# Second tokens' casts ahead of the first superblock's evictions, and two convolution parts in every step of the third superblock

## The chip, the cores and the metric

The kernel runs on one core of one Trainium2 chip. The metric is the device time of one execution in microseconds; the time before is the median of three runs. The profile is of one further execution.

## The reference

Eight sequences of 4096 tokens with 192 channels each go through a causal convolution of seven taps (a softmax of a learned weight per head, so one set of taps per channel), and the result goes through a two-layer network of 2048 hidden units with a squared ReLU between the layers:

```
w   = softmax(weight)                       # 8 heads x 7 taps, repeated over 24 channels each
x'  = sum over k of w[k] * x[t - 6 + k]     # zeros ahead of each sequence
h   = x' @ w_in                             # 32768 x 192 @ 192 x 2048
g   = s * relu(h)**2 + b
out = g @ w_out                             # 32768 x 2048 @ 2048 x 192, float32
```

## The kernel before

**Tiles.** The 32768 tokens are cut into 32 superblocks `n` of 1024 tokens, each of two blocks `j` of 512. The 2048 hidden units are cut into eight pairs `p` of 2 x 128. One step `(n, j, p)` computes the hidden units of pair `p` for one block. Channels lie on the partitions: 128 of them in an A tile, the other 64 in a B tile that holds both blocks' halves. Every float32 operand of a matmul is split into a high part and a low part, and three products (high x low, high x high, low x high) are accumulated.

**Work of a step.** `first(n, j, p)` issues 18 matmuls into `h` (line 547), in three groups of six: those on `sA`, then those on `tB` and `wB`, then those on `wA`. Here `sA` is the split A convolution, `wA` the same with its two partition halves exchanged, `tB` and `wB` the B convolution and its exchange. `relu` (L570) and `square` (L578) run on ScalarE; a cast to the high part (L580) on VectorE or ScalarE; the low part `ql` (L584) on VectorE. The results are put in a queue, and `second(...)` multiplies them by `w_out` two steps later (`LAG` is 2). For superblock 0 this is `second_whole` (L628 to L637), for superblock 1 `second_split` (L659), from superblock 2 on the loop of L714, with the last 64 output channels done for a whole superblock at once in `second_B` (L733), called by `batch(n - 1)` in step `(n, 0, 1)`.

**Evictions.** At `p` = 7 the accumulators leave PSUM: in superblock 0 by two ScalarE instructions and one VectorE instruction for each block (L641, L643, L645), in superblock 1 by four ScalarE instructions (L680, L683), later by L721 and L722. The output of superblock 0 and of block `(1, 0)` waits in SBUF for a bias that is known only in step `(2, 0, 0)`: `biases()` sums it with matmuls (L528) and VectorE (L530), GpSimd adds it to six tiles (L534), and these are written out (L535). The evictions of `(1, 1)` reuse the SBUF tiles of these outputs.

**The convolution ahead of time.** `Tokens(n).steps()` is a generator that issues the convolution and the casts of superblock `n` in small parts: for block 0 seven parts of the A convolution on VectorE (L174, L176) and two parts of its split (L191 on ScalarE; L193 on VectorE, with the exchange by DMA); then seven parts of the B convolution for both blocks and two or three parts of its split; then nine parts of the A tile of block 1. That is 27 parts for superblock 1, 28 for each other one, of which the first 19 are all that block 0 needs (the last of them exchanges `wB` by DMA, L184 and L185). For superblock 1 the B split is `split_B_at_once`: its first part casts the high part on ScalarE (L222), copies it into `tB` and `wB` (L227, twice) and subtracts on VectorE (L229, twice), and sets `begun`. `convolve(k)` issues the next `k` parts of the coming superblock; it stops early where a convolution ends, and the parts it still owes are added to the next call. `finish(block)` issues whatever parts are still missing for that block; every superblock calls it at the head of step `(n, j, 0)`.

**Order.** VectorE, ScalarE and TensorE run in the order in which the program names the instructions; a context called `in_order` fixes this. The loads of `x` are put as early in the SyncE queue as their buffers allow (`headed`), about two superblocks ahead. Superblock 0 is written out in `head()` and `pair(p)`; after `pair(7)` a loop issues the six outstanding `second_whole` groups, of which the last two carry the evictions of superblock 0. Then the steps of superblock 1 begin.

**What the counts give before.** When step `(2, 0, 0)` begins, 23 of the 28 parts of superblock 2 are issued. Its 16 steps call `convolve` with 1, 2, 1, 2 and so on, 24 parts in all: 5 for the rest of superblock 2, 19 for superblock 3. The 19th is issued in step `(2, 1, 7)`. From superblock 3 on, each superblock calls for 30 parts (`FIRST`), two more than the 28 needed.

Of the kernel before, what the change touches and what calls it, by code (L numbers as in the profile page):

```python
# [45 lines left out]
def conv_attention_then_squared_relu_mlp(  # L46
# [25 lines left out]
    NPAIR = weights64.shape[0]  # L72
# [308 lines left out]
    tok = {0: Tokens(0)}  # L381
# [117 lines left out]
    def column_sums(k):  # L499

        if k == 1:
            nc.gpsimd.memset(sumB[:, 0:DB], 0.0)
            for h in range(2):
                hi, lo = (splitB[h][:, :, k, :].bitcast(F32) for k in range(2))
                half = WB[:, h * NPAIR // 2 : (h + 1) * NPAIR // 2]
                nc.vector.tensor_tensor(half.rearrange("p a b d -> p (a b) d"), hi, lo, op=ALU.add)
        for o, w, w0 in (
            (sumA, W[:, k, :, CI:CB].bitcast(F32), W[:, 0, :, CI:CB].bitcast(F32)),
            (sumB[:, DB:].rearrange("p (j d) -> p j d", j=2), WB[:, k], WB[:, 0]),
        ):  # L510
            nc.vector.tensor_tensor(o, w0 if k == 1 else o, w, op=ALU.add)
        if k == NPAIR - 1:
            a, b = sumA, sumB
            nc.vector.tensor_tensor(a[:, 0, :], a[:, 0, :], a[:, 1, :], op=ALU.add)
            nc.vector.tensor_tensor(a[:, 0, 0:P], a[:, 0, 0:P], a[:, 0, P:], op=ALU.add)
            nc.vector.tensor_tensor(b[:, DB:P], b[:, DB:P], b[:, P:], op=ALU.add)
# [5 lines left out]
    def biases():  # L522

        pb = ps_h.tile([P, 2, BLK], F32, name="h")
        for k, cols in enumerate((sumA[:, 0, 0:P], sumB[:, 0:P])):
            for i in range(2):
                r = slice(i * HB, (i + 1) * HB)
                nc.tensor.matmul(pb[:, i, k : k + 1], cols[r], bb[r], start=True, stop=True)  # L528
        nc.scalar.copy(bias[:, 0:2], pb[:, 0, 0:2])
        nc.vector.tensor_tensor(bias[:, 0:2], bias[:, 0:2], pb[:, 1, 0:2], op=ALU.add)  # L530
        nc.vector.tensor_copy(bias[0:DB, 2:3], bias[DB:P, 1:2])
        for o, to, k in unbiased:
            rows = slice(0, o.shape[0])
            nc.gpsimd.tensor_scalar(o, o, bias[rows, k : k + 1], None, op0=ALU.add)  # L534
            nc.sync.dma_start(to, o)  # L535


    def first(n, j, p, meanwhile=None):
        h = ps_h.tile([P, 2, BLK], F32, name="h")
        halves = [tok[n].half(j, i) for i in range(2)]  # L540

        def both(w, part, at, start, stop):

            for i in range(2):
                chunk = halves[i][at]
                rows = slice(i * HB, (i + 1) * HB)
                nc.tensor.matmul(  # L547
                    h[:, i, :], w_in(w, p, chunk[0], rows), chunk[part], start=start, stop=stop
                )

        for at in (0, 2, 1):
            both(0, 1, at, at == 0, False)
            both(0, 2, at, False, False)
            both(1, 1, at, False, at == 1)
            if meanwhile and at == 0:
                meanwhile()
        return h
# [8 lines left out]
    def relu(h):  # L566
        g = count[0]
        count[0] += 1
        q = room_for(F32)
        nc.scalar.activation(q, h, AF.Relu)  # L570
        return q, g

    def squares(h, cast):
        return square(relu(h), cast)

    def square(at, cast):
        q, g = at
        nc.scalar.activation(q, q, AF.Square)  # L578
        qh, ql = split_place(g)
        cast(qh, q)  # L580
        return q, qh, ql
# [7 lines left out]
    def put(n, j, p, pair):  # L589
        if n >= OLD:  # L590
            kept[n, j, p] = pair[0]
        queue.append((n, j, p, *lows(*pair)))
# [3 lines left out]
    def banks():  # L596
        return [ps_o.tile([P, BLK], F32, name=f"acc{k}") for k in (1, 2)]
# [129 lines left out]
    def second_B(n, j, accs):  # L727

        for p in range(NPAIR):
            q = kept.pop((n, j, p))  # L730
            for r in (slice(0, HB), slice(HB, P)):
                for i in range(2):
                    nc.tensor.matmul(  # L733
                        accs[r.start // HB][i * DB : (i + 1) * DB], WB[r, p, i, :], q[r, i, :],
                        start=p == 0, stop=p == NPAIR - 1, skip_group_check=True,
                    )
        return accs
# [42 lines left out]
    def start_tokens(n):  # L780
        if n < NSUP:
            tok[n] = Tokens(n)
            tok[n].load()
# [7 lines left out]
    def convolve(k):  # L791


        k += owed[0]
        while k and coming[0] in tok:
            try:
                stop = next(tok[coming[0]].todo)
            except StopIteration:
                coming[0] += 1
                continue  # L800
            k -= 1
            if stop:
                break
        owed[0] = k if coming[0] in tok else 0

    def pair(p):

        ha, hb = first(0, 0, p), first(0, 1, p)
        if p + 1 < NPAIR:
            if p not in TWICE:  # L810
                wide[p + 1].rest()
            ahead, between = 0, CONV[p] // 4
        else:
            ahead, between = CONV[p] // 2, CONV[p] // 4
        convolve(ahead)
        def magnitudes():
            if p + 2 < NPAIR:
                wide[p + 2].magnitudes()

        qa = relu(ha)  # L820
        if p in TWICE:

            magnitudes()
            qb = relu(hb)
        qa = square(qa, nc.scalar.copy)
        if p not in TWICE:
            magnitudes()
        put(0, 0, p, qa)
        if p + 2 < NPAIR:
            wide[p + 2].top()  # L830
        convolve(between)
        if p not in TWICE:
            qb = relu(hb)
        qb = square(qb, nc.scalar.copy)
        if p + 2 < NPAIR:
            wide[p + 2].his()
        if p + 1 in TWICE:
            wide[p + 2].rest()
        put(0, 1, p, qb)
        convolve(CONV[p] - ahead - between)  # L840


    def batch(n):

        a = second_B(n, 0, banks())
        convolve(FIRST[2])
        evict_B(n, 0, a)
        a = second_B(n, 1, banks())
        convolve(FIRST[3])
        evict_B(n, 1, a)  # L850
# [3 lines left out]
    def step(n, j, p):  # L854
        if p == 0:
            tok[n].finish(j)
            if j == 0:
                with headed():
                    start_tokens(n + 1)
            else:  # L860
                tok.pop(n - 1)
        h = first(n, j, p)
        put(n, j, p, squares(h, nc.scalar.copy if n == OLD and p % 2 else nc.vector.tensor_copy))
        if (n, j) == (1, 1):
            if p < NPAIR - 1:
                column_sums(p + 1)
            convolve(1)
        elif n <= OLD:
            convolve(3 if n == 1 else 1 + p % 2)
        else:  # L870
            convolve(FIRST[p] if j == 0 and p < 2 else 1)
        if (n, j, p) == (2, 0, 0):
            biases()
        if (n, j, p) == steps[-1]:
            a = second_B(n, 0, banks())
            h = ps_h.tile([P, 2, BLK], F32, name="h")
            b = second_B(n, 1, [h[:, i, :] for i in range(2)])
            evict_B(n, 0, a)
            last_B(n, 1, b)
            for item in queue:  # L880
                second(*item)
        while queue and len(queue) > LAG + (
            queue[0][2] == 0 and queue[0][0] <= OLD and queue[0][:2] not in ((1, 0), (OLD, 1))
        ):
            if (n, j, p) == steps[-1]:
                break
            second(*queue.pop(0))
        if n > OLD and (j, p) == (0, 1):
            batch(n - 1)

    with in_order(nc.vector, nc.scalar, nc.tensor):
        with in_order(nc.sync):
            head()
        headed = last_of(nc.sync)
        for p in range(NPAIR):
            if p > 1:
                if p + 3 < NPAIR:
                    with headed():
                        fetch(p + 3)
                pair(p)  # L900
            if p > 0 and p not in TWICE:
                while len(queue) > (LAG if p < NPAIR - 1 else 0):
                    second(*queue.pop(0))
        for s_ in steps:
            if s_[0]:
                step(*s_)
# [43 lines left out]
```

## Time and profile before

| | |
|---|---|
| median of 3 runs | 2240.92 us (2239.67 to 2241.11) |
| the profiled execution's own time | 2240.58 us |
| span from its first to its last instruction | 2238.8 us |
| mean granted TensorE clock | 0.998 |
| TensorE matmuls busy | 2222.3 us (99%) |
| VectorE busy | 1734.5 us (77%) |
| ScalarE busy | 1315.0 us (59%) |
| GpSimd busy | 310.9 us (14%) |

In the profile PE is TensorE's matmuls and PEld its weight loads, DVE is VectorE, ACT is ScalarE, POOL is GpSimd, SP is SyncE, which issues the DMAs. A row of the timeline gives the start in us from the first instruction, the duration in us, engine, line, operation, what is written and read, the count of merged instructions, and in brackets the idle time of the engine just before with what ended it. A row of the chain of work that ended last gives start, duration, engine (or DMA), tile, line and count. A row of a stretch (from:to) gives its length, then the busy time and instruction count of PE, PEld, DVE, ACT and POOL, then the granted clock as a share of full speed, and the DMA share and rate.

### The profile page before, as it was taken

To read this page: it belongs to the slowest core of one execution; us is meant where nothing else is said; L and a number is where in the kernel's file an instruction comes from. 1 tells how busy PE (TensorE), PEld (TensorE's weight loads), DVE (VectorE), ACT (ScalarE), POOL (GpSimd) and SP (SyncE) were. 2 spreads that over 40 slices of the span, in tenths; PEclk is the share of its full clock that TensorE was granted. 3 is DMA by queue.
4 is the path that set the end of the run, shared out by engine and by line. 5 is a ranking of instruction groups with operands and counts; after the bars stand their busy time and mean duration, and the time that the engine had idled before them with its cause. 6 is when DMAs were issued, how large, how long until landed. Compare 5 with 4: busy or idle time off the path is not lost.

```text
span 2238.8 us, 44630 instructions
## 1 busy us (share of the span) xinstructions
PE 2222.3 (99%) x19334; PEld 1611.6 (72%) x19334; DVE 1734.5 (77%) x1988; ACT 1315.0 (59%) x1418; POOL 310.9 (14%) x205
## 2 busy tenths in 40 slices
PE   9998999999999999999999999999999999999999
PEld 6787667777777877777777777777777777777776
DVE  8797677877778787777887787877778877878754
ACT  8757555655555655556555566555565555665554
POOL 0013111011111111101111101111011111111110
PEclk9999999999999999999999999999999999999999
DMA  5012121112211111111112112121111121121110
GB/s 179 21 45 69 53 62 50 49 45 62 58 48 48 53 52 49 53 51 45 55 51 57 48 44 57 45 57 51 51 48 53 48 62 46 46 58 39 43 30 17
DMA packets 46165, 117.49 MB, mean 52 GB/s; under 512 B 7760, under 2 KB 8016, under 8 KB 45968
## 3 DMA queue, kind: packets, MB, share of 16 engines
q1 hardware_dynamic: 45824, 114.50, 18.4%
q8 instruction: 151, 2.47, 0.5%
q14 instruction: 46, 0.38, 0.1%
q10 hardware_dynamic: 144, 0.13, 0.0%
HBM read 31.64 MB, written 25.17 MB: 25 GB/s over the span
## 4 chain that ended last, share of the span: by engine, by line
PE 97%; DVE 2%; ACT 1%; DMA 0%; issue 0%; POOL 0%; SPq 0%; DVEq 0%; ACTq 0%
PE h L547 46%; PE acc L714 29%; PE acc L733 18%; PE acc L659 1%; PE acc L629 0%; PE acc L635 0%; PE acc L637 0%; PE h L733 0%; PE acc L636 0%; DVE accA L176 0%; DVE ql L584 0%; ACT q L570 0%; PE acc L628 0%; DMA wB<-tB 0%; PE acc L631 0%
## 5 line engine op out<-in xcount | busy, mean ns | idle before, releaser
L570 ACT ACTIVATE q<-h 128x1024 f32<-128x1024 f32 x512 | 526.4, 1028 | 580.1 <-PE h L547 579.0
L584 DVE TENSOR_TENSOR ql<-q,qh 128x1024 fp32r<-128x1024 f32 x498 | 663.9, 1333 | 60.2 <-ACT qh L580 9.1
L580 DVE CAST qh<-q 128x1024 fp32r<-128x1024 f32 x482 | 337.6, 700 | 379.3 <-ACT q L578 375.9
L714 PE MATMUL acc<-qh,W 64*128 64x512 f32 x3816 | 588.7, 387 | 1.5 <-ACT outs L680 1.5
L578 ACT ACTIVATE q<-q 128x1024 f32<-128x1024 f32 x512 | 543.6, 1062 | 16.0
L547 PE MATMUL h<-sA,W 64*128 64x512 f32 x3072 | 436.9, 389 | 0.0
L547 PE MATMUL h<-tB,W 64*128 64x512 f32 x1536 | 432.0, 387 | 4.7 <-DVE tB L208 2.8
L547 PE MATMUL h<-wB,W 64*128 64x512 f32 x1536 | 432.3, 388 | 4.2 <-DMA wB<-tB 4.1
L547 PE MATMUL h<-wA,W 64*128 64x512 f32 x3072 | 433.4, 387 | 0.0
L714 PEld LDWEIGHTS acc<-qh,W 64*128 64x128 f32 x3816 | 357.7, 184 | 78.2 <-ACT outs L680 1.9
L733 PE MATMUL acc<-q,WB 64*64 64x512 f32 x3776 | 412.1, 591 | 0.0
L714 PE MATMUL acc<-ql,W 64*128 64x512 f32 x1908 | 371.7, 386 | 0.6 <-DVE ql L584 0.6
L547 PEld LDWEIGHTS h<-sA,W 64*128 64x128 f32 x3072 | 285.8, 184 | 84.3 <-issue 24.7
L547 PEld LDWEIGHTS h<-wA,W 64*128 64x128 f32 x3072 | 289.1, 185 | 60.7
L733 PEld LDWEIGHTS acc<-q,WB 64*64 64x64 f32 x3776 | 141.5, 133 | 254.7 <-issue 254.7
L176 DVE SCALAR_TENSOR_TENSOR accA<-xA,tap,accA 128x512 f32<-128x512 f32 x378 | 315.8, 835 | 6.1
L547 PEld LDWEIGHTS h<-tB,W 64*128 64x128 f32 x1536 | 282.9, 184 | 46.3 <-DVE tB L208 3.3
L547 PEld LDWEIGHTS h<-wB,W 64*128 64x128 f32 x1536 | 283.0, 184 | 25.9 <-DMA wB<-tB 5.1
L723 POOL TENSOR_TENSOR outs<-outs 128x512 f32<-128x512 f32 x59 | 96.6, 1638 | 1242.0 <-ACT outs L722 1242.0
L714 PEld LDWEIGHTS acc<-ql,W 64*128 64x128 f32 x1908 | 179.0, 184 | 38.7 <-DVE ql L584 1.0
L176 DVE SCALAR_TENSOR_TENSOR accB<-xB,tap,accB 128x512 f32<-128x512 f32 x186 | 163.9, 881 | 5.6
L743 ACT ACTIVATE outs<-acc,bias,sb 128x512 f32<-128x512 f32 x59 | 45.9, 778 | 159.3 <-PE acc L733 159.3
(144 smaller groups left out, 959.1 us busy)
## 6 DMA issues: line engine op xcount, KB each, us to landing
wA<-sA SPq DMA_DIRECT2D x126, 256.0 KB, 3.7
outT<-outs SPq DMA_DIRECT2D x63, 256.0 KB, 2.0
wB<-tB SPq DMA_DIRECT2D x60, 256.0 KB, 3.4
xA<-in_xA SPq DMA_DIRECT2D x24, 515.0 KB, 3.6
outT<-outs SPq DMA_DIRECT2D x65, 128.0 KB, 2.3
xB<-in_xB SPq DMA_DIRECT2D x32, 259.0 KB, 3.0
outs<-outs SPq DMA_DIRECT2D x61, 128.0 KB, 2.4
outs<-in_w SPq DMA_DIRECT2D x7, 768.0 KB, 6.5
```

The source lines that it names most:

```text
L176: nc.vector.scalar_tensor_tensor(acc, src, w[:, k : k + 1], acc, op0=ALU.mult, op1=ALU.add)
L547: nc.tensor.matmul(h[:, i, :], w_in(w, p, chunk[0], rows), chunk[part], start=start, stop=stop)
L570: nc.scalar.activation(q, h, AF.Relu)
L578: nc.scalar.activation(q, q, AF.Square)
L580: cast(qh, q)
L584: nc.vector.tensor_tensor(ql, q, qh.bitcast(F32), op=ALU.subtract)
L659: nc.tensor.matmul(accs[to + 2 * i][0:cols], w(f, r), q[r, f % 2, :], start=start and f == 0, stop=stop and f == NF - 1,)
L714: nc.tensor.matmul(accs[i], w(f, r), q[r, f % 2, :], start=f == 0 and lo == 0, stop=f == ends[i] and lo == 2,)
L723: nc.gpsimd.tensor_tensor(o, o, o2, op=ALU.add)
L733: nc.tensor.matmul(accs[r.start // HB][i * DB : (i + 1) * DB], WB[r, p, i, :], q[r, i, :], start=p == 0, stop=p == NPAIR - 1, skip_group_c ...
L743: nc.scalar.activation(o, accs[0], AF.Identity, scale=sb, bias=bias[:, 1:2])
```

## The change

Two edits. In the loop over superblock 0's pairs, `tok[1].finish(0)` is called right after `pair(7)`, ahead of the loop that issues the last six `second_whole` groups; when step `(1, 0, 0)` calls it again, there is nothing left to do. The one part that it issues there is the first one of `split_B_at_once` (L222, L227 twice, L229 twice), since `pair(7)` has issued the whole B convolution already. And `convolve` in the steps of superblock 2 is called with 2 each time, 32 in all, instead of 1 and 2 in turn.

```
@@ step(n, j, p)
         elif n <= OLD:
-            convolve(3 if n == 1 else 1 + p % 2)
+            convolve(3 if n == 1 else 2)
@@ loop over the pairs of superblock 0
                 pair(p)
+            if p == NPAIR - 1:
+                tok[1].finish(0)
             if p > 0 and p not in TWICE:
                 while len(queue) > (LAG if p < NPAIR - 1 else 0):
                     second(*queue.pop(0))
```

By the counts, superblock 3 has 11 parts when block `(2, 1)` begins, its 19th is issued in step `(2, 1, 3)`, and 26 are issued when step `(3, 0, 0)` begins, with one owed.

More of the change, by code (lines that the diff above doesn't have):

```diff
@@ L868, in step @@
         elif n <= OLD:
-            convolve(3 if n == 1 else 1 + p % 2)
+            convolve(3 if n == 1 else 2)
         else:
@@ L900, in conv_attention_then_squared_relu_mlp @@
                 pair(p)
+            if p == NPAIR - 1:
+                tok[1].finish(0)
             if p > 0 and p not in TWICE:
```

## The prediction

> **What bounds the kernel.** I read the page first: busy times, then the chain of work that ended last. Then the stretches, to find where TensorE is not full.
>
> ```profile
> PE 2222.3 (99%) x19334; PEld 1611.6 (72%) x19334; DVE 1734.5 (77%) x1988; ACT 1315.0 (59%) x1418; POOL 310.9 (14%) x205
> PE 97%; DVE 2%; ACT 1%; DMA 0%; issue 0%; POOL 0%; SPq 0%; DVEq 0%; ACTq 0%
> 101.00:165.00 64.00, 64.00 (x570) 51.31 (x570) 60.43 (x85) 35.23 (x38) 5.10 (x3) 1.00 0.17 44
> 182.00:200.00 18.00, 18.00 (x162) 14.84 (x160) 14.56 (x17) 14.38 (x15) 1.61 (x1) 1.00 0.25 76
> ```
>
> TensorE is the bound, and the matmuls are not touched. So the change can win only in holes of PE: 2238.8 - 2222.3 = 16.5 us, and besides them the time that a lowered clock adds to busy matmuls. Three holes lie where the edits work, at 91, 173 and 219 us, and a small one at 468 us.
>
> **First edit, the casts at 88 to 94 us.**
>
> ```profile
> 68.18 0.97 PE L547 MATMUL h<-sA,W 64*128 64x512 f32 x6
> ...
> 69.67 0.86 PE L547 MATMUL h<-wA,W 64*128 64x512 f32 x6
> ...
> 87.68 0.74 DVE L176 SCALAR_TENSOR_TENSOR accB<-xB,tap,accB 128x512 f32<-128x512 f32 x1
> 88.46 0.69 ACT L641 ACTIVATE outs<-acc,sb 128x512 f32<-128x512 f32 x1 [1.96 <-PE acc L637]
> 90.62 0.97 PE L547 MATMUL h<-sA,W 64*128 64x512 f32 x6
> 92.15 0.62 ACT L222 CAST hiB<-accB 128x512 fp32r<-128x512 f32 x1
> 93.44 0.62 ACT L227 CAST wB<-hiB 64x512 fp32r<-64x512 f32 x1
> 93.47 0.50 PE L547 MATMUL h<-tB,W 64*128 64x512 f32 x1 [1.88 <-ACT tB L227]
> 96.91 1.02 ACT L570 ACTIVATE q<-h 128x1024 f32<-128x1024 f32 x1 [2.85 <-PE h L547]
> 101.28 0.39 PE L659 MATMUL acc<-qh,q 64*128 64x512 f32 x2
> 95.00:96.00 1.00, 1.00 (x8) 0.84 (x6) 0.00 (x0) 0.00 (x0) 0.00 (x0) 0.50 0.00 0
> ```
>
> The B convolution ends at 87.68 + 0.74 = 88.42, but ScalarE does four evictions from 88.46 on, and the casts start only at 92.15. TensorE has its six `sA` matmuls from 90.62, then stands 1.88 us, and afterwards runs at clock 0.50. With the edit L222 starts at 88.46. The three casts take 92.15 to 94.06, 1.9 us; so `tB` and `wB` are cast by 90.4, and the two subtractions on VectorE, which start when L222 ends, are done by then too. TensorE asks for them at 91.4 (0.8 us after 90.62): no wait, and no clock loss. Undisturbed, a `first` takes 69.67 + 0.86 - 68.18 = 2.35 us to its last result, so `h` is complete at 92.97. Late next are the evictions: the four take 92.15 - 88.46 less the idle 0.88 between them, 2.8 us, and now end at 90.4 + 2.8 = 93.2. The ReLU queued behind them starts at 93.2 and not at 96.91: 3.7 us earlier. VectorE's two L645 end by 94; what follows on VectorE waits for the square at 95.3. The accumulators that the evictions free are wanted at 96.8 (90.62 + three `first` of 2.04). No DMA moves: the first part of this split exchanges nothing.
>
> The bounds: all that is lost here is 101.28 - 96.8 = 4.5 us; nothing, if VectorE (60.43 of 64.00 us busy behind it) is already the pace. I take 3.7, since the ReLU releases ScalarE, VectorE and so TensorE alike, and all three move by it.
>
> **Second edit, the hole at 219 to 232 us.** In the chain:
>
> ```profile
> 212.14 2.04 PE h L547 x18
> ...
> 215.54 2.06 PE h L547 x18
> ...
> 224.32 3.46 DMA wB<-tB
> ...
> 232.01 2.07 PE h L547 x18
> ```
>
> A step takes 215.54 - 212.14 = 3.40 us. Two steps after 215.54 would be 222.34; the trace has 232.01: 9.7 us are lost, to the last B parts (issued in step (2,1,7)), their exchange by DMA and the clock after it. With two parts in each step the 19th part falls into (2,1,3), four steps or 13.6 us earlier, against a lateness of 9.7. All 9.7 go. The exchanges move in SyncE's queue by as much; they are 3.46 us each and have 10 us to spare, even behind an output that waits. The `x` loads only come earlier, as their buffers come free.
>
> Eight parts more run in this superblock, and eight fewer later. Behind 182 us VectorE works 14.56 of 18.00 us, 2.75 us in a step of 3.40. One more part in every second step adds half of 0.75, giving 3.1: it fits. What if not, see below.
>
> **The hole at 468 us.** The `second_B` batches mark the superblocks in the chain; the last row is from the view of who waited for whom, PE alone, 235 to 2200 us:
>
> ```profile
> 372.66 13.89 PE acc L733 x128
> ...
> 441.22 13.89 PE acc L733 x128
> ...
> 510.78 13.89 PE acc L733 x128
> PE acc L714 <- DVE ql L584: 0.6, 1, 0.6
> ```
>
> 68.56 us is the rule, but 69.56 the one from 441.22. There, in step (6,0,2), seven parts come at once, two of a split and five of a convolution, because `convolve` stopped at a convolution's end before and owed the rest. The wait for `ql` is the only one of L714 behind 235 us. By the count, the lead of two parts per superblock makes this pattern in superblock 6 alone; with eight parts more, superblock 3 enters as superblock 7 does now, all but one part, and superblocks 4 on are as 8 on are now, which take 68.56. Gain 1.0 (bounds 0 and 1.0).
>
> **What the second edit costs at 166 to 186 us.**
>
> ```profile
> 165.91 0.74 DVE L176 SCALAR_TENSOR_TENSOR accA<-xA,tap,accA 128x512 f32<-128x512 f32 x1
> 166.57 0.15 DVE L530 TENSOR_TENSOR bias<-bias,h 128x2 f32<-128x2 f32 x1
> 166.82 10.64 POOL L534 TENSOR_SCALAR outs<-outs,bias 128x512 f32<-128x512 f32 x6 [26.13 <-DVE bias L530]
> 172.34 0.78 ACT L680 ACTIVATE outs<-acc,bias,sb 128x512 f32<-128x512 f32 x1 [2.53 <-DMA outT<-outs]
> 174.41 0.73 PE L714 MATMUL acc<-qh,W 64*128 64x512 f32 x4 [1.50 <-ACT outs L680]
> 177.44 1.72 POOL L684 TENSOR_TENSOR outs<-outs 128x512 f32<-128x512 f32 x1
> 178.04 2.19 DVE L584 TENSOR_TENSOR q<-q 128x1024 fp32r<-128x1024 f32 x1
> 179.12 2.27 POOL L688 TENSOR_TENSOR outs<-outs 128x512 f32<-128x512 f32 x1
> 180.59 1.88 DVE L584 TENSOR_TENSOR ql<-q,qh 128x1024 fp32r<-128x1024 f32 x1 [0.35 <-ACT qh L580]
> 181.72 1.90 POOL L693 TENSOR_TENSOR outs<-outs 64x512 f32<-64x512 f32 x1 [0.29 <-DMA outs<-outs]
> 182.40 1.77 DVE L193 TENSOR_TENSOR sA<-accA,sA 128x512 fp32r<-128x512 f32 x1
> 183.87 0.39 PE L714 MATMUL acc<-ql,W 64*128 64x512 f32 x2
> 193.66 1.23 DVE L584 TENSOR_TENSOR ql<-q,qh 128x1024 fp32r<-128x1024 f32 x1 [1.33 <-ACT qh L580]
> 201.60 0.68 DVE L193 TENSOR_TENSOR sA<-accA,sA 128x512 fp32r<-128x512 f32 x1
> 173.00:174.00 1.00, 0.00 (x0) 0.00 (x0) 0.00 (x0) 1.00 (x3) 1.00 (x1) 1.00 0.63 248
> 279.57 1.79 DVE L176 SCALAR_TENSOR_TENSOR accB<-xB,tap,accB 128x512 f32<-128x512 f32 x1
> ```
>
> Times here are those of the trace before, the 3.7 left out. First, in step (2,0,0) a second L176 stands ahead of the bias addition L530. It delays L530, and with it POOL's additions, the output's DMA, the evictions L680 and the matmuls at 174.41, by 0.75 us: the hole becomes 2.3 us.
>
> Second, the split L193 and the first part of the next A convolution (L174) move from behind the L584 at 180.59 to ahead of it. POOL works there. L193 took 1.77 beside POOL, 0.68 alone. After its predecessor ends at 178.04 + 2.19 + 0.75 = 181.0, I let L193 wait for L688 (181.39 + 0.75) and end at 182.8, L174 wait for L693 and end at 184.3, and L584 end at 185.5. TensorE wants this `ql` at 183.87 + 0.75 = 184.6: 0.9 us lost. Uncontended L584 would end at 181.0 + 0.7 + 0.5 + 1.2 = 183.4 and nothing would be lost. The Trainium skill, "SBUF — State Buffer", section "Who interferes with whom", says that a VectorE instruction with two SBUF inputs and a GpSimd instruction that reads SBUF exclude each other for the whole instruction; by it the loss is the 0.9, without it 0, and the 1.77 against 0.68 agrees with it. Later steps absorb the rest: the added part sits where VectorE stands idle 1.33 us.
>
> Cost 0.75 + 0.9 = 1.7 (bounds: 0.7 and 4.1, the latter with the clock of the third rival).
>
> **The sum.** -3.7 - 9.7 - 1.0 + 1.7 = -12.7 us. The profiled execution took 2240.58, 0.3 below the median and 1.8 above its span; so 2227.9 against it, and 2228.2 against the median of 2240.92. I forecast 2228.
>
> **Rivals.** 0.2% of this time, 4.5 us, is about what a measurement can tell from no change: the line is 2236.4.
> 1. VectorE is the pace of superblock 1, and the first edit gives nothing: 60.43 of 64 us speaks for it; against it, TensorE is full throughout. 2228 + 3.7 = 2232.
> 2. VectorE falls behind in parts of superblock 2 (each added part unabsorbed, 8 x 0.75 = 6): 2234. The idle 1.33 speaks against it.
> 3. The longer hole at 173 lowers the clock. After 1.50 us of idleness it stayed 1.00, after 1.88 us at 91 it fell to 0.50, so 2.3 us may trip it. The price by the rows of 91 us is what that hole lost beyond the wait: 4.5 - (93.47 - 91.4) = 2.4, giving 2230.6; most of it runs beside the `ql` waits above, so nearer to 2229. The Trainium skill, "TensorE: Matmul & The Clock Gate", section "What's actually happening", lets the clock fall only after an idle window of about 3.4 us. By that rule 2.3 us trips nothing and the sum stays; the fall after 1.88 us disagrees with so long a window.
> 4. Slower: VectorE saturates over the whole of superblock 2 through contention with POOL. The tipping point is 6.8 us of VectorE work in two steps; it is 5.5 now and 6.25 with the change, so four parts would have to cost 0.14 us more each. At the 1.79 of the row at 279.57 each costs 1.04 more: 6.25 + 4.2 - 6.8 = 3.6 us for each of 8 pairs of steps, 29 us lost; 2240.6 + 29 - 3.7 - 9.7 - 1.0 = 2255. Against it: POOL is busy 1.61 of 18.00 us behind 182.
> 5. The edit does nothing at 88 us because the casts are not what TensorE waits for: the row at 93.47 names L227, so this is the first rival's time again.
>
> **Chances.** The forecast with or without the third rival, 2226 to 2230.6: 0.72. First (and fifth): 0.11. Second: 0.08. Some of these together, up to 2237: 0.06. Fourth: 0.03. The range from 2225.5 to 2234 leaves out less than 2 in 10. Faster by over 0.2%: 0.92; within: 0.05; slower: 0.03.
>
> **What would show it.** L222 ahead of L641 and no wait of PE at `tB` near 91, the clock at 1.00 from 94 to 98; near 217 us (219 less 3.7, plus 1.7) no wait for `tB` or `wB` and steps of 3.40 through into superblock 3; the PE wait behind L680 longer than 1.50 and a new wait for `ql` some 10 us later; all batches 68.56 apart. A VectorE wait of PE in every step from 180 to 215, or in superblock 1, would make the prediction wrong.

## The result, and the profile after

The changed kernel takes 2227.94 us (median of 6 runs, 2226.98 to 2228.08) against 2240.84 us (median of 6, 2239.67 to 2241.11): ratio 0.9942, 95% interval 0.9929 to 0.9955. It is 12.9 us faster, and 2228 was forecast. Its profiled execution took 2227.96 us, span 2226.2 us, mean clock 0.999.

The page, first the busy times:

```profile
PE 2218.1 (100%) x19334; PEld 1610.4 (72%) x19334; DVE 1744.4 (78%) x1988; ACT 1314.9 (59%) x1418; POOL 309.6 (14%) x205
```

TensorE now leaves 2226.2 - 2218.1 = 8.1 us idle, where it left 16.5. The rest of the gain is in the busy time, 2218.1 us where it was 2222.3 for the same 19334 matmuls: a matmul at the lowered clock counts as busy, and for longer (the four of L714 behind the hole at 172 us take 1.22 us at the low clock here, 0.73 at the full one in e4 below).

The casts at 88 us, in the timeline of ScalarE and TensorE (start, duration, engine, line, what, count, idle time before), with the clock at 95 us from the stretches and the start of superblock 2 from the chain of work that ended last:

```profile
88.61 0.62 ACT L222 CAST hiB<-accB 128x512 fp32r<-128x512 f32 x1 [1.96 <-DVE accB L176]
89.91 0.62 ACT L227 CAST wB<-hiB 64x512 fp32r<-64x512 f32 x1
90.55 0.69 ACT L641 ACTIVATE outs<-acc,sb 128x512 f32<-128x512 f32 x1
90.79 0.97 PE L547 MATMUL h<-sA,W 64*128 64x512 f32 x6
91.60 0.39 PE L547 MATMUL h<-tB,W 64*128 64x512 f32 x1
93.46 1.03 ACT L570 ACTIVATE q<-h 128x1024 f32<-128x1024 f32 x1
95.00:96.00 1.00, 1.00 (x12) 0.81 (x10) 0.39 (x1) 0.97 (x2) 0.00 (x0) 1.00 0.00 0
156.26 2.06 PE h L547 x18
```

The casts stand ahead of the evictions L641, the matmul on `tB` has no idle time in brackets, the clock stays at 1.00, and the ReLU starts at 93.46 instead of 96.91. The first step of superblock 2, which began at 159.74 before, begins at 156.26; this execution was 0.17 late already at the `sA` matmuls (90.79 against 90.62), so the edit brings 3.48 + 0.17 = 3.65 us.

The hole where superblock 2 begins, in the timeline and the stretches (from:to, length, busy time and count of PE, PEld, DVE, ACT, POOL, then the granted clock):

```profile
163.88 0.15 DVE L530 TENSOR_TENSOR bias<-bias,h 128x2 f32<-128x2 f32 x1
169.67 0.78 ACT L680 ACTIVATE outs<-acc,bias,sb 128x512 f32<-128x512 f32 x1 [3.33 <-DMA outT<-outs]
171.75 1.22 PE L714 MATMUL acc<-qh,W 64*128 64x512 f32 x4 [2.30 <-ACT outs L680]
172.00:173.00 1.00, 1.00 (x6) 0.81 (x8) 0.00 (x0) 1.00 (x2) 1.00 (x2) 0.50 0.35 84
175.00:176.00 1.00, 1.00 (x12) 0.84 (x10) 0.97 (x2) 0.97 (x2) 1.00 (x2) 0.91 0.37 86
177.34 1.51 POOL L693 TENSOR_TENSOR outs<-outs 64x512 f32<-64x512 f32 x1 [0.72 <-DMA outs<-outs]
177.62 1.77 DVE L193 TENSOR_TENSOR sA<-accA,sA 128x512 fp32r<-128x512 f32 x1
178.21 1.53 PE L714 MATMUL acc<-q,W 64*128 64x512 f32 x12
179.71 1.21 DVE L584 TENSOR_TENSOR ql<-q,qh 128x1024 fp32r<-128x1024 f32 x1
182.06 0.40 PE L714 MATMUL acc<-ql,W 64*128 64x512 f32 x2
178.00:196.00 18.00, 18.00 (x162) 15.42 (x160) 16.30 (x20) 13.59 (x14) 0.84 (x1) 1.00 0.38 104
```

The idle time behind L680 is 2.30 us (1.50 before), and now the clock falls to 0.50 for a good 3 us behind it. The wait for `ql` that the prediction placed here is not there: L584 ends at 179.71 + 1.21 = 180.92, and TensorE takes its result at 182.06. Behind that, VectorE works 16.30 of 18.00 us, 3.08 us in a step of 3.40, without holding up TensorE.

Step (2,0,5), the start of superblock 3, and the batches that mark the superblocks, in the chain:

```profile
179.74 2.04 PE h L547 x18
...
213.74 2.04 PE h L547 x18
220.54 2.04 PE h L547 x18
223.94 13.89 PE acc L733 x128
...
429.58 13.89 PE acc L733 x128
498.14 13.89 PE acc L733 x128
```

The steps of 3.40 run through (213.74 to 220.54 are two). The step that began at 215.54 before begins at 213.74, 1.80 ahead; the one of 232.01 begins at 220.54, 11.47 ahead: 9.67 us came from here. From 429.58 to 498.14 is 68.56, where the same superblock took 69.56: 1.0 more.

### The profile page after: what moved, and what is told of

The parts are those of the page before. It is cut to its first block, busy times and chain, and to the rows that moved or that the text cites. A ratio compares the mean times of both kernels' runs of the same rounds, so it can differ in the third digit from the quotient of the medians.

```text
span 2226.2 us, 44633 instructions
## 1 busy us (share of the span) xinstructions
PE 2218.1 (100%) x19334; PEld 1610.4 (72%) x19334; DVE 1744.4 (78%) x1988; ACT 1314.9 (59%) x1418; POOL 309.6 (14%) x205
## 4 chain that ended last, share of the span: by engine, by line
PE 97%; DVE 2%; ACT 1%; DMA 0%; issue 0%; POOL 0%; SPq 0%; DVEq 0%; ACTq 0%
PE h L547 46%; PE acc L714 29%; PE acc L733 18%; PE acc L659 1%; DVE accA L176 0%; DVE ql L584 0%; PE h L733 0%; ACT q L578 0%; ACT q L570 0%; PE acc L629 0%; PE acc L635 0%; PE acc L637 0%; PE acc L636 0%; DMA xA<-in_xA 0%; POOL outs L534 0%
## 5 line engine op out<-in xcount | busy, mean ns | idle before, releaser
L584 DVE TENSOR_TENSOR ql<-q,qh 128x1024 fp32r<-128x1024 f32 x498 | 669.6, 1345 | 55.6 <-ACT qh L580 4.3
L714 PE MATMUL acc<-qh,W 64*128 64x512 f32 x3816 | 589.3, 387 | 2.3 <-ACT outs L680 2.3
L547 PE MATMUL h<-sA,W 64*128 64x512 f32 x3072 | 436.3, 389 | 0.0
L547 PE MATMUL h<-wA,W 64*128 64x512 f32 x3072 | 432.0, 386 | 0.0
L547 PE MATMUL h<-tB,W 64*128 64x512 f32 x1536 | 430.3, 386 | 0.0
L547 PE MATMUL h<-wB,W 64*128 64x512 f32 x1536 | 430.3, 386 | 0.0
L714 PEld LDWEIGHTS acc<-qh,W 64*128 64x128 f32 x3816 | 358.1, 184 | 78.6 <-ACT outs L680 2.7
L714 PE MATMUL acc<-ql,W 64*128 64x512 f32 x1908 | 372.0, 386 | 0.0
L547 PEld LDWEIGHTS h<-sA,W 64*128 64x128 f32 x3072 | 285.4, 184 | 84.0 <-issue 24.7
L547 PEld LDWEIGHTS h<-wA,W 64*128 64x128 f32 x3072 | 288.1, 184 | 60.4
L176 DVE SCALAR_TENSOR_TENSOR accA<-xA,tap,accA 128x512 f32<-128x512 f32 x378 | 313.4, 829 | 5.7
L547 PEld LDWEIGHTS h<-tB,W 64*128 64x128 f32 x1536 | 282.6, 184 | 40.4 <-issue 0.2
L547 PEld LDWEIGHTS h<-wB,W 64*128 64x128 f32 x1536 | 282.5, 184 | 20.7
L723 POOL TENSOR_TENSOR outs<-outs 128x512 f32<-128x512 f32 x59 | 94.9, 1608 | 1226.7 <-ACT outs L722 1226.7
L714 PEld LDWEIGHTS acc<-ql,W 64*128 64x128 f32 x1908 | 179.2, 184 | 37.6
L176 DVE SCALAR_TENSOR_TENSOR accB<-xB,tap,accB 128x512 f32<-128x512 f32 x186 | 167.4, 900 | 6.3
L745 POOL TENSOR_TENSOR outs<-outs 128x512 f32<-128x512 f32 x59 | 108.5, 1839 | 199.8 <-ACT outs L744 199.5
```

Of the source, the lines that this page charges most:

```text
L176: nc.vector.scalar_tensor_tensor(acc, src, w[:, k : k + 1], acc, op0=ALU.mult, op1=ALU.add)
L547: nc.tensor.matmul(h[:, i, :], w_in(w, p, chunk[0], rows), chunk[part], start=start, stop=stop)
L584: nc.vector.tensor_tensor(ql, q, qh.bitcast(F32), op=ALU.subtract)
L714: nc.tensor.matmul(accs[i], w(f, r), q[r, f % 2, :], start=f == 0 and lo == 0, stop=f == ends[i] and lo == 2,)
L723: nc.gpsimd.tensor_tensor(o, o, o2, op=ALU.add)
L745: nc.gpsimd.tensor_tensor(o, o, o2, op=ALU.add)
```

## The experiments

Each was timed beside the kernel before. Times are medians.

**e1 and e2: each edit alone.** e1 has the call of `finish` but keeps the old counts; e2 has the new counts without the call.

```
e1, against the changed kernel:
-            convolve(3 if n == 1 else 2)
+            convolve(3 if n == 1 else 1 + p % 2)
e2, against the changed kernel:
-            if p == NPAIR - 1:
-                tok[1].finish(0)
```

> Only the casts ahead of superblock 0's evictions; superblock 2 keeps 1 and 2 parts in turn. If the edits add up as the prediction's terms do: no wait of PE for tB near 91 us, superblock 2 begins 3.5 us earlier than before, the holes at 173 (1.50 us, clock 1.00), at 219 and at 468 us stay, and the time is 2240.8 - 3.6 = 2237.2 (range 2236.7 to 2237.8). If the first edit gains nothing, because VectorE is the pace of superblock 1: 2240.8. If the whole loss of 4.5 us comes back: 2236.3.

> Only the two parts in every step of superblock 2; the casts stay behind the evictions. If the edits add up: the wait for tB near 91 us and the low clock behind it as before, the hole behind L680 longer by 0.8 us, 9.7 us gained at 219 and 1.0 at 468 us, 1.7 lost near 170 to 180: 2240.8 - 9.0 = 2231.8 (range 2231.2 to 2232.5). If the clock's fall in the longer hole depends on what ran before, it may not fall here; then the loss near 175 is 0.8 and the time 2230.9.

e1: 2237.68 us (2236.51 to 2238.21) against 2240.75, ratio 0.9987 (0.9977 to 0.9996), 3.1 us faster, the 3.6 expected lying within the spread of its runs. e2: 2230.73 us, ratio 0.9957 (0.994 to 0.9974), 10.0 us faster. Together 13.1, where the whole change brought 12.9: the edits add up, to within about 1 us, as e2's profile will show. In e1 the waits for `wB` and `tB` near 219 us stay (view of who waited for whom, PE: total, times, longest):

```profile
PE h L547 <- DMA wB<-tB: 4.1, 2, 3.7
PE h L547 <- DVE tB L208: 2.8, 1, 2.8
PE acc L714 <- ACT outs L680: 1.5, 1, 1.5
```

e2 came out 1.1 us below what was expected of it, and below the range given. Up to 158 us its program is that of before, and in its profiled execution TensorE waits just as long for the casts, but the clock at 95 us is 1.00. In the longer hole behind L680 it did fall (row at 176):

```profile
93.49 0.49 PE L547 MATMUL h<-tB,W 64*128 64x512 f32 x1 [1.89 <-ACT tB L227]
95.00:96.00 1.00, 1.00 (x12) 0.83 (x10) 0.00 (x0) 0.16 (x1) 0.00 (x0) 1.00 0.00 0
158.65 2.06 PE h L547 x18
176.00:177.00 1.00, 1.00 (x8) 0.76 (x6) 0.31 (x1) 1.00 (x2) 1.00 (x2) 0.50 0.04 12
```

Superblock 2 begins at 158.65, 159.74 before: the fall of the clock cost 1.1 us there and is not in every execution. The four runs fit this: the three with a mean clock of 0.999 took 2230.36 to 2230.75, the one with 0.998 took 2231.63. The expectation's other way to such a time (2230.9, no fall in the longer hole) is ruled out by the row at 176. The 3.65 us of the first edit are therefore about 2.5 for the wait and 1.1 for the clock. In the profiled execution of e2 the 1.1 came without the first edit, so the sum of e1 and e2 can count it twice.

**e3 and e4: what the start of superblock 2 costs.** e3 issues one part and not two in step (2,0,0), so that the bias addition has only one L176 ahead of it. e4 leaves the change as it is and fills the hole with two matmuls that add zeros to `h` (four in the trace).

```
e3:
-            convolve(3 if n == 1 else 2)
+            convolve(3 if n == 1 else 1 if (j, p) == (0, 0) else 2)
e4, after first(2, 0, 3):
+        if (n, j, p) == (2, 0, 3):
+            for _ in range(2):
+                nc.tensor.matmul(h[0:DB, 0, :], sumB[:, 0:DB],
+                    sumB[:, 0:1].to_broadcast([P, BLK]), start=False, stop=True, ...)
```

> The changed kernel, but step (2,0,0) issues one part instead of two, so the bias addition L530 is not delayed; 31 parts in superblock 2. Theory, clock: the hole behind L680 is back at 1.50 us, the clock stays at 1.00, and the step (2,0,5) begins 1.7 us earlier than in the changed kernel, less any wait for ql: 2226.2 to 2226.6. Theory, port: the loss of 0.9 us is VectorE's, in the wait for ql of step (2,0,3), whatever the clock; then only the 0.8 of the hole comes back, a wait of PE for ql of 0.5 us or more shows near 180, and the time is 2227.1.

> The changed kernel with two matmuls of zeros (64 x 512, float32) added into h after first(2,0,3), where PE otherwise waits 2.3 us for L680; they add zero to h. Theory, clock: the fall to 0.50 follows the idleness of PE, so with the hole filled the clock stays at 1.00 from 172 to 176 us, second(2,0,0) starts at the same 171.7, and (2,0,5) begins about 0.9 us earlier, limited then by ql of (2,0,2): 2227.0. Theory, evictions alone: the loss comes from the late evictions and VectorE, not from the clock; no change, 2227.9 (or up to 0.5 more, if the zeros delay the matmuls behind them).

e3: 2226.83 us, ratio 0.9938 (0.9923 to 0.9953). e4: 2227.09 us, ratio 0.9939 (0.9925 to 0.9954). In e4 the L714 behind the hole begins when it did in the changed kernel, but at full clock (timeline and stretch):

```profile
169.56 1.94 PE L865 MATMUL h<-sumB 128*64 128x512 f32 x4
171.93 0.73 PE L714 MATMUL acc<-qh,W 64*128 64x512 f32 x4 [0.43 <-ACT outs L680]
173.00:174.00 1.00, 1.00 (x12) 0.84 (x10) 0.00 (x0) 0.97 (x2) 1.00 (x2) 1.00 0.68 262
177.96 1.19 PE L714 MATMUL acc<-q,W 64*128 64x512 f32 x8 [0.52 <-DVE q L584]
```

So the fall of the clock costs 0.85 us, by the medians of 2227.94 and 2227.09 (2227.0 was expected of e4). The spread of the changed kernel's own runs fits this: the four with a mean clock of 0.999 take 2227.94 to 2228.08, the two with 1.000 take 2226.98 and 2227.18. The low clock by itself costs more: the L714 behind the hole and what follows take 4.42 us up to the next L547 in the changed kernel, 2.85 in e4. But TensorE, so late, then finds VectorE's result ready at its next L714 (178.21 above, no idle time in brackets), where it waits 0.52 us in e4 (177.96) and 0.35 in the kernel before (timeline):

```profile
180.29 1.21 PE L714 MATMUL acc<-q,W 64*128 64x512 f32 x8 [0.35 <-DVE q L584]
```

In e3, whose time lies between the two that its expectation gave, the hole is 1.52 us again, the clock stays up, and TensorE now waits for the `ql` that the prediction named:

```profile
178.44 2.31 DVE L584 TENSOR_TENSOR ql<-q,qh 128x1024 fp32r<-128x1024 f32 x1
180.81 0.50 PE L714 MATMUL acc<-ql,W 64*128 64x512 f32 x2 [0.19 <-DVE ql L584]
```

L584 takes 2.31 beside GpSimd and 1.21 in the changed kernel. With it, e3 needs 25.70 us from the start of superblock 2 to step (2,0,6) and the kernel before 25.20, so this wait and the restart behind it cost 0.5. The clock is not what keeps it out of the changed kernel: in e4 the clock is up, TensorE comes earlier, and this `ql`, ready at 181.12, is taken without a wait at 181.49. What differs is GpSimd. Its six additions L534 take 10.64 us in e3, as before, but 9.52 in the changed kernel and 9.53 in e4, so that there its last piece of work (L693) ends at 177.34 + 1.51 = 178.85, ahead of L584 at 179.71. In e3 L693 starts at 178.29 and runs beside L584. Why L534 is shorter, no run isolates.

**e5, e6 and e9: taking the cost away.** e5 moves `biases()` ahead of `convolve`. e6 adds to it that the output which gates L680 first is written out first (the two tiles of a block change places in the list, and GpSimd's additions keep the list's order). e9 is e6 with the same 32 parts spread differently, none in the steps (2,0,2) and (2,0,3), where GpSimd still works. In e6 and e9 the lines named here behind L530 have numbers one higher.

```
e5:
+        if (n, j, p) == (2, 0, 0):
+            biases()
...
-        if (n, j, p) == (2, 0, 0):
-            biases()
e6, besides:
-            unbiased.append((oA, outT[0:P, t0 : t0 + BLK], 0))
...
+            unbiased.append((oA, outT[0:P, t0 : t0 + BLK], 0))
+        with in_order(nc.gpsimd):
e9, besides:
-            convolve(3 if n == 1 else 2)
+            convolve(3 if n == 1 else 0 if (j, p) in ((0, 2), (0, 3)) else 2 + j * (p % 2))
```

> The changed kernel with biases() called ahead of convolve in step (2,0,0), so that both L176 stand behind L530. L530 then starts 1.4 us earlier than in the changed kernel. Theory, the hole is set by the chain L530, POOL, DMA, L680: the hole behind L680 shrinks from 2.30 to 0.9 us, the clock stays at 1.00, the matmuls of L714 start at 170.3 and (2,0,5) 6.9 us behind them, at 177.2 against 179.6: 2227.9 - 2.1 = 2225.8 (range 2225.4 to 2226.3; a wait for ql beside POOL of up to 0.5 is in it). Rival, the hole is set by something else (the accumulators' own matmuls or ScalarE): hole and time hardly move, 2227 to 2228.

> As e5, and the B output of superblock 0, whose tile the first eviction of (1,1) takes over, gets its bias first on POOL instead of second (superblock 0's two outputs change places in the list, and POOL follows the list). Theory, chain: one POOL addition of 1.6 us less before L680; it starts at 166.7, when ScalarE is free, no hole of PE behind (2,0,3) is left, (2,0,5) begins near 175.9, with one wait for ql of (2,0,2) of some 0.5 us: 2227.9 - 3.6 = 2224.3 (range 2223.8 to 2225.0). Rival, VectorE and POOL become the pace there: the matmuls start early but wait for ql by as much, 2225.5 or more.

> The kernel of e6 with the same count of convolution parts in superblock 2 differently spread: none in steps (2,0,2) and (2,0,3), where GpSimd works, three instead of two in the odd steps of block 1 (32 parts as before, the 19th in step (2,1,4), three steps ahead of its use). Theory, that VectorE beside GpSimd is the pace in e6: its two waits for ql of 0.29 and 0.59 us and the weight-load wait behind them go, about 1.5 us, so 2225.7 - 1.5 = 2224.2 (2223.7 to 2225.0), with no wait of PE for ql between 170 and 185 us. Rival, that the three-step lead is too short or VectorE has no room for three parts in block 1: a wait of PE for wB or tB near 213 us takes it back, 2225.5 or more.

e5: 2225.71 us against 2240.97, ratio 0.9934 (0.992 to 0.9947); 2225.8 was expected. The bias addition comes 1.84 earlier than in the changed kernel, 1.4 of it by the edit (superblock 2 begins 0.40 earlier in this execution), and the hole shrinks to 1.20 us:

```profile
162.04 0.15 DVE L530 TENSOR_TENSOR bias<-bias,h 128x2 f32<-128x2 f32 x1
170.24 0.74 PE L714 MATMUL acc<-qh,W 64*128 64x512 f32 x4 [1.20 <-ACT outs L680]
```

e6: 2225.68 us, ratio 0.9933 (0.992 to 0.9947); 2224.3 was expected, and the rival came true. The wait behind L680 (L681 here) is gone, but what was saved is lost to VectorE. Its L193 and L174 still lie in GpSimd's time, L174 with 1.51 us instead of the 0.47 of the changed kernel, and TensorE now waits twice for `ql`:

```profile
174.02 1.78 DVE L193 TENSOR_TENSOR sA<-accA,sA 128x512 fp32r<-128x512 f32 x1
175.73 1.51 DVE L174 TENSOR_SCALAR accA<-xA,tap 128x512 f32<-128x512 f32 x1
178.43 0.50 PE L715 MATMUL acc<-ql,W 64*128 64x512 f32 x2 [0.29 <-DVE ql L585]
182.85 0.50 PE L715 MATMUL acc<-ql,W 64*128 64x512 f32 x2 [0.59 <-DVE ql L585]
221.46 13.89 PE acc L734 x128
```

e9: 2224.10 us against 2240.74, ratio 0.9926 (0.9912 to 0.9939), and 2224.2 was expected: the fastest version here. L193 and the parts behind it are moved out of GpSimd's time, and L193 takes 0.68; the two L585 that remain beside GpSimd (the first is not shown) take 2.2 and hold up nothing. Both waits for `ql` are gone, and the first batch begins 1.60 before e6's:

```profile
178.30 2.20 DVE L585 TENSOR_TENSOR ql<-q,qh 128x1024 fp32r<-128x1024 f32 x1
180.42 0.68 DVE L193 TENSOR_TENSOR sA<-accA,sA 128x512 fp32r<-128x512 f32 x1
219.86 13.89 PE acc L734 x128
```

**e7: the hole at 468 us by itself.** The kernel before, with two parts in each step of block (3,1), so that superblock 4 gets its lead one superblock after the place where the change gives it.

```
-            convolve(FIRST[p] if j == 0 and p < 2 else 1)
+            convolve(FIRST[p] if j == 0 and p < 2 else 2 if (n, j) == (3, 1) else 1)
```

> The kernel before, with neither edit, but two parts instead of one in the steps (3,1,p), eight parts more in superblock 3. The holes at 91, 173 and 219 us stay. If the hole at 468 us comes from the seven parts at once that the lead of 25 parts gives in (6,0,2): it is gone, all batches from superblock 4 on are 68.56 us apart, and the time is 2240.8 - 1.0 = 2239.8. If it belongs to superblock 6 for another reason: still one gap of 69.56, 2240.8. If eight parts more cost something where nothing else is going on: over 2240.8.

e7: 2239.76 us against 2240.97, ratio 0.9995 (0.9986 to 1.0004); 2239.8 was expected, but by time alone this is inconclusive. In its chain the superblock that took 69.56 takes 68.56:

```profile
442.71 13.89 PE acc L733 x128
511.27 13.89 PE acc L733 x128
```

**e8: fewer steps of lead.** Block (2,0) keeps 1 and 2, only block (2,1) gets two parts in each step; the 19th part falls into (2,1,5) and not (2,1,3).

```
-            convolve(3 if n == 1 else 2)
+            convolve(3 if n == 1 else 2 if j else 1 + p % 2)
```

> The changed kernel, but the two parts in every step only in block 1 of superblock 2; block 0 keeps 1 and 2 in turn. 28 parts: the 19th of superblock 3 falls into step (2,1,5), two steps ahead of its use instead of four, and 23 are issued when superblock 3 begins. By the prediction's terms: the hole at 173 stays 1.50 with the clock at 1.00, so nothing of the 1.7 is paid; the hole at 219 is gone (6.8 us of lead, and the last parts need about 5: L208, L209 and a DMA of 3.46); and a gap of 69.56 appears at superblock 4, where the lead passes 25. 2240.8 - 3.6 - 9.7 = 2227.5 (range 2226.9 to 2228.0). If two steps are too short a lead: a wait for wB near 217 us, up to 2230.

e8: 2228.98 us against 2240.97, ratio 0.9948 (0.9935 to 0.9962), slower than the 2227.5 expected. The exchange comes too late:

```profile
214.07 3.58 DMA wB<-tB
216.42 0.49 PE L547 MATMUL h<-wB,W 64*128 64x512 f32 x1 [0.38 <-DMA wB<-tB]
217.70 0.50 PE L547 MATMUL h<-wB,W 64*128 64x512 f32 x1 [0.78 <-DMA wB<-tB]
```

It lands at 217.65. In the changed kernel the same DMA is issued at 209.24, lands by about 212.7 at such a duration and is first read at 217.65 (timeline of SyncE and TensorE):

```profile
209.24 1.05 SPq L184 DMA_DIRECT2D wB<-tB  x1
217.65 0.39 PE L547 MATMUL h<-wB,W 64*128 64x512 f32 x1
```

It has 5 us to spare there; two steps less of lead are 6.8 us, so e8 had to wait. As e8's expectation said, a long superblock appears as well, superblock 4 with 69.64 us between the batches at 292.49 and 362.13.

## Why the prediction was right

Three of the four terms of the sum came as told. The fourth, the cost at the start of superblock 2, has the right size by luck.

- **First edit: -3.7, measured -3.65.** L222 stands at the end of the B convolution, there is no wait for `tB`, and the ReLU comes 3.5 us earlier. The split of the 4.5 us between the wait and the clock was wrong: 2.4 for the clock in the prediction, 1.1 by e2. The first rival (VectorE the pace of superblock 1) and the fifth are refuted by the same 3.65.
- **Hole at 219: -9.7, measured -9.67.** The parts moved four steps, and all of the loss went. The 9.7 was read from the execution that it is measured against; in the profiled executions of e1 and e7, which keep this hole, it cost 10.0 and 11.1. The spare of the exchange was put at 10 us and is 5; that changed nothing here, but e8 shows where it ends.
- **Hole at 468: -1.0, measured -1.0**, by the chain of the changed kernel and of e7.
- **VectorE in superblock 2:** 3.1 us in a step was forecast, 3.08 measured, and no wait of TensorE. The second rival is out. So is the fourth: GpSimd was busy only 0.84 of those 18.00 us.
- **The cost at the start of superblock 2: +1.7, measured 3.48 - 1.77 = 1.71**, as step (2,0,5), which began at 181.51 before (chain of before, below), begins at 179.74. The first term, the later bias addition, is 0.75 in the prediction and 2.30 - 1.50 = 0.8 in the trace. The second term, a wait of TensorE for `ql` of 0.9, failed: it did not come, since GpSimd was done before that L584 began, and the fall of the clock, the third rival, put 0.9 in its place (0.85 by e4). That the two amounts are alike is luck. With the clock up and the same parts (e4) the second term would have been about 0.1: from the start of superblock 2 to step (2,0,6) e4 takes 26.11 us, 0.9 more than the 25.20 of the kernel before, of which the hole is 0.8. Where the wait does come, in e3, it costs 0.5. The working of the 0.9 also has a slip: its L693 ends at 181.72 + 1.90 + 0.75 = 184.37, so an L174 that waits for it cannot end at 184.3, and by those steps the loss would be some 1.5. The third rival was priced at 2.4 by the rows at 91 us, with most of it beside the `ql` wait, "nearer to 2229". What it swallowed was the wait for VectorE one step earlier, which the kernel before has too and which the prediction's lines do not show.

```profile
181.51 2.07 PE h L547 x18
```

By the chains, the changed kernel is 3.48 us ahead where superblock 2 begins, 1.77 at step (2,0,5), 11.47 at the step of 220.54 and 510.78 - 498.14 = 12.64 behind the superblock that was too long. The profiled executions differ by 2240.58 - 2227.96 = 12.6, the medians by 12.9.

## What to carry to other kernels

The time that TensorE loses to a low clock and its wait for the next engine don't add up: here the clock took up a wait of 0.52 us, so price each alone, and charge the larger where they stand in the same steps. When a term is removed, ask at once what stands behind it; here the hole, the clock and the VectorE instructions beside GpSimd were three layers, worth 2227.94 - 2224.10 = 3.8 us together (the hole with the 1.50 us that the kernel before has), and e5 and e6, which took away one or two of them, did not get it all. Work that must be ready in time can be shifted among steps, as in e9, as long as it keeps its lead, which e8 lost; count the lead from the landing of the last transfer.

## What the runs showed of the hardware

Whether the clock falls is not the same in every execution. Behind idle times of TensorE of 1.88 to 2.30 us it fell to 0.50 in some executions and not in others of the same program: with 1.89 us at 91 us it stayed up in e2, where it fell in the kernel before with 1.88 (for 2.30 the execution without a fall is inferred from the mean clock of 1.000). With the holes of 1.52 and 1.20 us in e3 and e5 the mean clock is 1.000 in all their runs. The price was 1.1 and 0.85 us. The Trainium skill, "TensorE: Matmul & The Clock Gate", section "What's actually happening", gives an idle window of about 3.4 us before the clock falls; falls behind 1.88 and 2.30 us disagree with it as a lower bound on one idle stretch.

The stretches show also how long the clock stays low. Behind these single holes it was 3.4 us each time: worked out from the partly low rows, from 94.32 to 97.74 in the kernel before, 171.76 to 175.18 in the changed one, 175.09 to 178.50 in e2. Behind the hole at 219 us it was 6.8 us in the kernel before and in e1, and 10.1 in e7 (223.91 to 234.03), whose program is that of before up to there. So a hole's price differs by execution, and e7's profiled execution, 2241.13 us, is the longest of its ten.

VectorE's subtraction L193 took 1.77 and 1.78 us beside GpSimd and 0.68 alone, and the subtraction L584 2.2 to 2.3 against 1.21. The Trainium skill, "SBUF — State Buffer", section "Who interferes with whom", has two-input VectorE instructions and GpSimd's reads lock each other out; the traces agree that such an instruction takes longer beside GpSimd. The one-input L174 took longer there too, 1.51 us in e6 against 0.47. e9 shows what it is worth to move the convolution's VectorE work out of two steps, L193 and L174 among it: 1.6 us between e6's and e9's first batches.
